# A planned order of work laid out anew: load times in the plan, the last step's product order, and the table of urgency shifts

## The chip, the cores and the metric

The kernel runs on one core of a Trainium2 chip. A core has five engines that work side by side, each through its own instructions in order: TensorE (matmuls into PSUM), VectorE and ScalarE (element by element), GpSimd (POOL in the profile), and SyncE (SP), whose queue here issues nearly all DMAs. The metric is the device time of one execution in microseconds; less is better. The program is one launch, and all loops are unrolled when it is built.

## The reference

Two blocks in a row, in float32. First a linear attention with decay (RWKV-6) for 4 batches, 8 heads, 768 steps, head width 48; then, over the heads laid side by side (384 wide), a layer norm and an MLP with a ReLU and a residual:

```
state = 0                                   # per batch and head, 48 x 48
for t in range(768):
    cur   = outer(u * k[t], v[t])
    y[t]  = r[t] @ (state + cur)
    state = w[t][:, None] * state + outer(k[t], v[t])
x   = y, heads side by side                 # (4, 768, 384)
xn  = (x - mean(x)) / sqrt(var(x) + 1e-6) * g_ln
out = x + max(xn @ w_ch1, 0) @ w_ch2        # w_ch1: 384 x 1536, w_ch2: 1536 x 384
```

## The kernel before

The work is cut into eight rounds, numbered 0 to 7: for each of the four batches two halves of 384 steps (RN). A round has three tiles of 128 steps (TT) and two units of four heads each (U). Round 0 is cut once more, into its first tile and the other two, so that work can start early.

A round's attention (`front`, line 1559 on) loads w, k, r and v, transposes w, k and r on TensorE (`turn`, tensors `w_ps`, `k_ps`, `r_ps`), and turns the recurrence into products inside chunks of 64 steps plus a state carried from chunk to chunk. Inside a chunk six levels (`quads`, `grow`, `keep`) alternate between many small matmuls that share the array (the "packed" groups, written to tensors called `a`) and VectorE, which multiplies k and r by decays (`tot`) and keeps the right squares under a mask. `states` computes the carried states, `outputs` the y, and `own` with `own_term` the term with u. In rounds 0 and 1 the loads put rows together in another way, so this last term goes through DRAM once (`own_by_tile`: `own_row` to `own_d` to `own`).

Then come the layer norm (`normalize`, `turn_x`) and the MLP (`first_product` for round 0, `mlp` for the others). The first product of a round has 12 parts f of 128 columns, the second adds 12 parts into three output tiles. To take fewer passes on TensorE than plain float32 does, operands are split into a high part, a low part and a difference: from round 1 on in the first product (`xhl`, `xd`, `wh`, `wl`, `d`), and in the last three rounds, 5 to 7, also in the second (`thirds`). There each f brings to each of the three output tiles i a product D of the differences (into one PSUM bank), and a product L and a product H (into another). For i = 0 and 1 the two banks are the two halves of one tile `a`; for i = 2 they are two tiles, `o_2D` and `o_2P`. Behind the last f VectorE adds D to x (`add`), then L + H to x (`rest`), and SP stores the tile (`store`).

What sets the order is the class `Plan` (line 67 on). The code above does not emit instructions; it calls `plan.add` with an engine, an assumed cost, the keys read and written, and an urgency `pri` (a smaller number goes first). The urgency of stage s in round n is 40n + s; MLP products lie 200 higher, so they fill in where the attention has nothing ready. `Plan.order` then plays through all operations: at each engine, among the operations that could start within WAIT of the earliest, it picks the one with the smallest urgency. The order in which it picks is the order of the program: each engine works through it, and waits where an input isn't there. So costs and urgencies in the plan have an effect on the chip through the order alone.

These parts matter here:

- `SHIFTS`: a table that adds a number to the urgency of all operations whose urgency has a given whole part. `MARGIN` is the delay assumed between an input and a packed group behind the first 60 us (FILLED); `PATIENCE` is how long GpSimd may be held for VectorE's shared port; `STAY` is a penalty on changing between packed and plain matmuls; `FETCH` the assumed time to fetch instructions; `WAIT` the window above, for each engine.
- `lat` is what the plan adds between an operation's end and the use of its result; for loads `size` is the time that the transfer takes up the DMA engines in the plan.
- `load` (line 494 on): rounds 0 and 1 (`ROWS`) take one DMA for each tensor and unit, later rounds three, one for each tile. The plan's cost for the three is 1.65, their latency 2.0. `load_v` (line 827 on) has the same latency.
- In `thirds` (line 1336 on), `go_d` issues the one matmul of D, `go` the two of L and H, `both` all three, in this order, as one planned operation of cost 0.525; its urgency is 200 + 40n + 2f + 3, which is 505 for the last f (11) of the last round.
- `idle` (line 1656 on) lets TensorE multiply zeros where the plan has a gap of more than 0.4 us in the first 90 us.

Of the kernel before, what the change touches and what calls it, by code (L numbers as in the profile page):

```python
# [35 lines left out]
class InOrder:  # L36


    waits, last = [], None
# [27 lines left out]
class Plan:  # L67
# [11 lines left out]

    HOP, MARGIN, FILLED, PATIENCE, STAY = 0.1, 0.196918, 60.0, 4.33011, 6.79752
    BEFORE, PIECE, FETCH, CROWD = 66, 256, 3.98109, 300
    WAITS = 1.006
    DRAIN = {True: 0.1, False: 0.12}
    WAIT = {"PE": 0.0354766, "ACT": 0.217982, "DVE": 0.140393, "POOL": 0.485775, "SP": 0.0207245}

    SHIFTS = {  # L90
        -537: -0.5, -535: -6.5, -520: -4, -457: -8, -337: 9.5, -296: 10.5, -295: 5.5, -200: -2,
        -38: -71, -34: 42.5, -31: -47, -30: -6.5, -29: 16, -25: -3, -18: -10.5, -14: -56, 0:
        -25, 6: -19.5, 8: -4, 9: -2.5, 10: -43, 11: 16, 12: -24, 14: 3, 16: 18, 17: 31, 26: -27,
        46: 6.5, 50: -49, 52: 46.5, 61: -28.5, 64: 5.5, 66: 11, 68: -8, 86: 5.5, 91: -28, 96:
        -20.5, 98: -50, 102: 40.5, 110: 4.5, 121: -4, 122: 14, 125: -0.5, 127: -9, 131: -17.5,
        136: -30, 140: 24.5, 165: -9, 166: -6, 168: -11.5, 172: -40, 174: -34.5, 178: -1.5, 180:
        -14.5, 182: 25.5, 202: 4.5, 203: 37, 204: -10, 210: -66.5, 212: -41, 260: -1.5, 261:
        -16.5, 280: 30, 283: -13, 284: -4.5, 310: 5, 319: -7.5, 320: 9, 402: 6, 407: -20.5, 409:
        -6, 411: -30, 418: -9.5, 425: 2.5, 440: -68, 442: 5, 443: 5.5, 444: -9.5, 450: -20.5,
        453: 38, 459: -24, 463: 40.5, 480: 3.5, 481: 3, 483: 9.5, 486: -3.5, 490: 3.5, 495: 15,  # L100
        496: 18, 497: 17.5, 499: 64.5, 501: 5,
    }

    def __init__(self, homes, dynamic):
# [37 lines left out]
    def order(self, busy, idle=None, until=0.0):  # L142
# [49 lines left out]
        def switching(t, op):  # L192
            drain = self.DRAIN[op.tiled] * (op.tiled != tiled)
            waits = fetches(t + drain, op)[0] > 2 * self.DRAIN[True]
            return self.STAY * (op.tiled != tiled) + self.CROWD * waits

        while todo:
            best = None
            for e, waiting in ready.items():
                at = [(t, op) for op in waiting if (t := start_of(op, e)) is not None]  # L200
                if not at:
                    continue
                first = min(t for t, _ in at)
                t, op = min(
                    ((t, op) for t, op in at if t <= first + self.WAIT[e]),
                    key=lambda x: (x[1].pri + (switching(*x) if e == "PE" else 0), x[1].i),
# [74 lines left out]
def kernel(  # L281
# [13 lines left out]
    PE, ACT, DVE, POOL, SP = (  # L295
        InOrder(tc, e) for e in (nc.tensor, nc.scalar, nc.vector, nc.gpsimd, nc.sync)
    )
# [8 lines left out]
    U = H // NH  # L306
# [11 lines left out]
    NR = B * NHALF  # L318
# [17 lines left out]
    plan = Plan(HOMES | {"a": 2, "b": 4}, ("a", "b"))  # L336
# [27 lines left out]
    ROWS, ROW = 2, TT * D  # L364
# [64 lines left out]
    def at(rnd, stage):  # L429
        return 40 * rnd + stage  # L430
# [13 lines left out]
    def urgent(part, stage):  # L444
        rnd, c0, nc = part
        return at(rnd - (nc == 1), stage)
# [47 lines left out]
    def load(nm, q):  # L494
        b, f, g = units[q]
        name = f"nat_{nm}{q}"

        def go():
            to = tile_("nat", name, None)
            if q // U < ROWS:  # L500
                SP.dma_start(
                    out=to[:, 0 : NH * ROW].rearrange("p (h x) -> p h x", h=NH),
                    in_=SRC[nm][b, ts(g, NH), ds(f * RN, RN)]
                    .rearrange("h (p c) d -> p h (c d)", p=P),
                )
                return
            for c in range(TT):
                SP.dma_start(
                    out=by_tile(to)[:, c, :, 0:D],
                    in_=SRC[nm][b, ts(g, NH), ds(f * RN + c * P, P)].rearrange("h p d -> p h d"),  # L510
                )

        cost_, size = (0.5, 1.05) if q // U < ROWS else (1.65, 1.6)
        plan.add(
            "SP", cost_, go, w=[name], new=[("nat", name)], pri=at(q // U, "wrk".index(nm)), lat=2.0,
            size=size,
        )

    def by_tile(t):
        return t.rearrange("p (c h d) -> p c h d", c=TT, h=NH)  # L520
# [306 lines left out]
    def load_v(q, part):  # L827
        _, c0, nc = part
        b, f, g = units[q]
        name, swapped = f"v{q}", f"vx{q}"  # L830

        def go():
            t = tile_("v", name, [P, NH, TT, D])
            for c in range(c0, c0 + nc):
                SP.dma_start(
                    out=t[:, :, c],
                    in_=v[b, ts(g, NH), ds(f * RN + c * P, P)].rearrange("h p d -> p h d"),
                )

        def swap():  # L840
            t, src = tile_("vx", swapped, [P, NP, TT, D]), tiles[name]
            cols = slice(c0 * D, (c0 + nc) * D)
            for i in range(2):
                SP.dma_start(
                    out=t[ds(C * (1 - i), C)].rearrange("p r c d -> p r (c d)")[..., cols],
                    in_=src[ds(C * i, C)]
                    .rearrange("p (r j) c d -> p r j (c d)", j=2)[:, :, 1, cols],
                )

        share = nc / TT  # L850
        plan.add(
            "SP", 0.1 + 1.6 * share, go, w=[(name, c0)], new=[] if c0 else [("v", name)],
            pri=urgent(part, 16), lat=2.0, size=1.6 * share,
        )
        plan.add(
            "SP", 1.3, swap, r=[(name, c0)], w=[(swapped, c0)], new=[] if c0 else [("vx", swapped)],
            pri=urgent(part, 17), lat=2.2, size=0.2 + 0.5 * share,
        )
# [477 lines left out]
    def thirds(rnd, f):  # L1336

        x_, h_, (g, c) = f"x{rnd}", f"h{rnd}_{f}", divmod(f, KC + 1)
        b, f0 = rounds[rnd]
        H_, L_, D_ = (f"h{n}{rnd}_{f}" for n in "HLD")  # L1340
        pri = at(rnd, FILL) + 2 * f + 3

        def out_tiles(i):
            if i < 2:
                t = tile_("a", f"o{rnd}_{i}", None)
                return t[:, 0, 0:RN], t[:, 1, 0:RN]
            return [tile_("b", f"o{rnd}_{i}{n}", [P, RN]) for n in "PD"]
# [21 lines left out]
        first, last = f == 0, f == FC - 1  # L1369
        whole = x_of(rnd)  # L1370
        for i in range(TT):
            o = f"o{rnd}_{i}"
            names = [o] if i < 2 else [o + "P", o + "D"]

            def go_d(i=i):
                PE.matmul(
                    out_tiles(i)[1], tiles[D_][:, ts(i, P)], tiles[f"w2d{f}"], start=first, stop=last
                )

            def go(i=i):  # L1380
                to = out_tiles(i)[0]
                PE.matmul(
                    to, tiles[L_][:, ts(i, P)], tiles[f"w2l{g}"][:, c], start=first, stop=False
                )
                PE.matmul(
                    to, tiles[H_][:, ts(i, P)], tiles[f"w2h{g}"][:, c], start=False, stop=last
                )

            def both(i=i):
                go_d(i)  # L1390
                go(i)

            def add(i=i):
                x = tiles[x_][:, i]
                DVE.tensor_tensor(
                    out=x, in0=out_tiles(i)[1].rearrange("p (h d) -> p h d", d=D), in1=x, op=ALU.add
                )

            def rest(i=i):
                x = tiles[x_][:, i]  # L1400
                DVE.scalar_tensor_tensor(
                    out=x, in0=out_tiles(i)[0].rearrange("p (h d) -> p h d", d=D),
                    scalar=1.0 + E12, in1=x, op0=ALU.mult, op1=ALU.add,
                )

            def store(i=i):
                SP.dma_start(
                    out=out[b, ds(f0 * RN + i * P, P), :].rearrange("t (h d) -> t h d", d=D),
                    in_=tiles[x_][:, i],
                )  # L1410

            keys = [o + n if i == 2 else (o, n) for n in "PD"]
            need = [H_, L_, D_, f"w2d{f}", (f"w2h{g}", c), (f"w2l{g}", c)]
            if first:
                need += x_of(NR - 1)
            plan.add(
                "PE", 0.525, both, count=6, r=need, w=keys,
                new=[("a" if i < 2 else "b", n) for n in names] if first else [],
                pri=pri, lat=0.17,
            )  # L1420
            if last:
                plan.add("DVE", 0.53, add, r=[keys[1]] + whole, w=[(x_, "sum", i)], pri=EVICT)
                plan.add("DVE", 0.53, rest, r=[keys[0], (x_, "sum", i)], w=[(x_, "out", i)], pri=EVICT)
                plan.add("SP", 0.36, store, r=[(x_, "out", i)], pri=EVICT, lat=2.0, size=0.65)
# [134 lines left out]
    def front(part):  # L1559
# [26 lines left out]
        if rnd:  # L1586
            for q in qs:
                load("r", q)
# [39 lines left out]
    def back(rnd):  # L1628
# [5 lines left out]
        w=["g"], pri=-10, lat=2.0, size=0.2,  # L1634
# [63 lines left out]
```

## Time and profile before

| | |
|---|---|
| median of 3 runs | 527.17 us (525.99 to 527.70) |
| profiled execution | 526.92 us |
| its span | 525.2 us |
| TensorE busy | 515.8 us (98%), 8996 matmuls in the records |
| VectorE busy | 403.6 us (77%) |
| ScalarE busy | 269.8 us (51%) |
| GpSimd busy | 72.2 us (14%) |
| DMA | 55.84 MB, mean 106 GB/s |
| granted TensorE clock | 1.00 |

The profile is of one execution. The span runs from the first to the last instruction; the time of the execution has some 1.7 us more around it. Names in its lines are the program's: `nat<-in_r_dram` is a load of r, `r_ps` the transposed r, `a<-r,k` packed squares, `idle<-nought` the multiplied zeros, `x<-a,x` an addition into the output. All instructions carry line 50, that of a helper that records them, so one goes by the names. "idle before <-releaser" is time in which the engine had nothing running, and what ended it. A matmul's end is modelled, and matmuls overlap: neighbours of 128 x 384 start about 0.175 us apart, though each is shown with 0.33 us and more.

### The profile page before, as it was taken

The page shows a single profiled execution, that of the slowest core. Times are in us where ns is not written, and L with a number is a line of the kernel's source. Part 1 is how long each engine was busy: PE and PEld are TensorE (multiplying, and loading weights), DVE is VectorE, ACT ScalarE, POOL GpSimd, SP SyncE. Part 2 cuts the span into 40 slices and gives each one's busy share as a digit, 9 for nine tenths or more (in the row PEclk, how much of TensorE's full clock was granted, in tenths as well). Part 3 has the DMA queues.
Part 4 walks back from the last instruction along what each step waited for, and adds up shares of the span by engine and source line. Part 5 has one row for each costly group of instructions (what it writes and reads, how often), then busy time and mean ns, then how long its engine had stood idle before and what let it go on. Part 6 is the DMA issues. An engine that isn't in the chain of part 4 may idle for free.

```text
span 525.2 us, 20616 instructions
## 1 busy us (share of the span) xinstructions
PE 515.8 (98%) x8996; PEld 434.5 (83%) x8996; DVE 403.6 (77%) x845; ACT 269.8 (51%) x602; POOL 72.2 (14%) x106
## 2 busy tenths in 40 slices
PE   9999999999999999999999999999999999999996
PEld 6788788677998668989777898669967999999996
DVE  5899988998899998999893886736664855855645
ACT  3788978973584244385451395246731524332221
POOL 7311311100420012223120010001500000000000
PEclk9999999999999999999999999999999999999999
DMA  9958595087545724655712311404101322322201
GB/s 215 273 158 205 119 232 163 18 208 209 143 83 102 187 50 93 145 121 102 174 39 67 78 38 25 133 22 120 47 16 61 107 61 65 101 60 85 83 0 46
DMA packets 122362, 55.84 MB, mean 106 GB/s; under 512 B 93984, under 2 KB 119200, under 8 KB 122272
## 3 DMA queue, kind: packets, MB, share of 16 engines
q1 hardware_dynamic: 119152, 53.54, 40.3%
q10 hardware_dynamic: 3120, 0.98, 1.0%
q8 instruction: 71, 1.16, 0.9%
q14 instruction: 19, 0.16, 0.1%
HBM read 45.05 MB, written 7.10 MB: 99 GB/s over the span
## 4 chain that ended last, share of the span: by engine, by line
PE 88%; DMA 4%; DVE 3%; POOL 2%; ACT 1%; issue 0%; SPq 0%; POOLq 0%; DVEq 0%
PE a L50 24%; PE o L50 23%; PE h_ps L50 21%; PE hd_ps L50 9%; PE o_2P L50 2%; PE w_ps L50 2%; PE r_ps L50 2%; DMA nat<-in_w_dram 2%; PE kn_ps L50 2%; PE k_ps L50 2%; PE xT_ps L50 1%; PE o_2D L50 1%; DVE x L50 1%; DMA own<-own_d 1%; DVE w L50 1%; POOL wide L50 1%
## 5 line engine op out<-in xcount | busy, mean ns | idle before, releaser
L50 PE MATMUL o<-ffn,h 128*128 128x384 f32 x360 | 124.4, 490 | 0.0
L50 PEld LDWEIGHTS o<-ffn,h 128*128 128x128 f32 x360 | 65.7, 190 | 37.5
L50 ACT COPY h<-hd_ps 128x384 f32<-128x384 f32 x84 | 40.3, 479 | 80.0 <-PE hd_ps L50 77.4
L50 DVE SCALAR_TENSOR_TENSOR h<-h_ps,h 128x384 f32<-128x384 f32 x84 | 46.5, 555 | 42.1 <-PE h_ps L50 38.1
L50 PEld LDWEIGHTS a<-r,k 48*60 48x60 f32 (+5 forms) x4608 | 63.3, 126 | 15.4 <-issue 7.4
L50 PE MATMUL a<-r,k 48*60 48x32 f32 (+5 forms) x4608 | 69.6, 212 | 0.9 <-issue 0.6
L50 PE MATMUL h_ps<-xhl,wl 128*128 128x384 f32 x252 | 61.1, 350 | 0.0
L50 PE MATMUL h_ps<-xhl,wh 128*128 128x384 f32 x252 | 57.6, 337 | 0.0
L50 PE MATMUL hd_ps<-xd,d 128*128 128x384 f32 x252 | 57.2, 348 | 0.0
L50 DVE TENSOR_TENSOR k<-k,tot 112x768 f32<-112x768 f32 (+1 forms) x50 | 41.7, 833 | 16.7 <-PE a L50 13.9
L50 PEld LDWEIGHTS hd_ps<-xd,d 128*128 128x128 f32 x252 | 44.2, 188 | 1.6 <-ACT w L50 0.2
L50 PEld LDWEIGHTS h_ps<-xhl,wl 128*128 128x128 f32 x252 | 43.8, 188 | 1.8 <-DVE h L50 0.2
L50 PEld LDWEIGHTS h_ps<-xhl,wh 128*128 128x128 f32 x252 | 45.2, 188 | 0.0
L50 ACT ACTIVATE h<-h 128x384 f32<-128x384 f32 x48 | 25.1, 525 | 33.3 <-DVE h L50 32.7
L50 DVE TENSOR_TENSOR r<-r,tot 112x768 f32<-112x768 f32 (+1 forms) x50 | 40.3, 807 | 0.0
L50 DVE COPY_PREDICATED A<-mask,a 128x768 f32<-128x768 int8 (+2 forms) x36 | 39.3, 1091 | 0.5 <-PE a L50 0.3
L50 ACT ACTIVATE hH<-h 128x384 fp32r<-128x384 f32 x36 | 18.4, 524 | 30.2 <-DVE h L50 25.8
L50 ACT COPY A<-a 32x384 f32<-32x384 f32 (+2 forms) x36 | 15.5, 432 | 26.9 <-PE a L50 25.7
L50 DVE SCALAR_TENSOR_TENSOR hL<-h,hH 128x384 fp32r<-128x384 f32 x36 | 19.9, 553 | 9.8 <-ACT hH L50 9.7
L50 PE MATMUL h_ps<-xf,w 128*128 128x128 f32 (+1 forms) x144 | 26.2, 331 | 0.0
L50 PE MATMUL a<-w2d,hD 128*128 128x384 f32 x72 | 24.6, 342 | 0.7 <-DVE hD L50 0.7
L50 PEld LDWEIGHTS a<-v,A 64*64 64x64 f32 x384 | 20.5, 133 | 5.4 <-issue 2.0
(121 smaller groups left out, 1000.8 us busy)
## 6 DMA issues: line engine op xcount, KB each, us to landing
d<-w1d SPq DMA_DIRECT2D x84, 192.0 KB, 2.9
raw<-in_moe_w_ch_dram SPq DMA_DIRECT2D x24, 384.0 KB, 4.7
v<-in_v_dram SPq DMA_DIRECT2D x48, 96.0 KB, 2.8
out_dram<-x SPq DMA_DIRECT2D x24, 192.0 KB, 1.9
nat<-in_w_dram SPq DMA_DIRECT2D x36, 96.0 KB, 3.5
nat<-in_k_dram SPq DMA_DIRECT2D x36, 96.0 KB, 3.6
nat<-in_r_dram SPq DMA_DIRECT2D x36, 96.0 KB, 3.1
w1d<-w1diff SPq DMA_DIRECT2D x12, 192.0 KB, 2.7
```

The costliest lines, as they stand in the source:

```text
L50: ins = self.tc.keep_in_program_order(f(*args, **kw))
```

## The change

Three things change, and with the third some constants of the planner. The plan's cost of a group of three loads goes from 1.65 to 1.95 and their latency from 2.0 to 2.5 (rounds 2 to 7); that of `load_v` from 2.0 to 2.5 in all rounds. In the last f of the last round, the three D products are planned as operations of their own, with an urgency lower by 100, and the L and H products as others. The table SHIFTS is replaced, 92 entries by 60, and MARGIN, PATIENCE, STAY, FETCH and WAIT have new values.

```diff
-    HOP, MARGIN, FILLED, PATIENCE, STAY = 0.1, 0.196918, 60.0, 4.33011, 6.79752
-    BEFORE, PIECE, FETCH, CROWD = 66, 256, 3.98109, 300
+    HOP, MARGIN, FILLED, PATIENCE, STAY = 0.1, 0.05, 60.0, 15.1983, 20.0356
+    BEFORE, PIECE, FETCH, CROWD = 66, 256, 3.72835, 300
...
-    WAIT = {"PE": 0.0354766, "ACT": 0.217982, "DVE": 0.140393, "POOL": 0.485775, "SP": 0.0207245}
+    WAIT = {"PE": 0.0403625, "ACT": 0.191784, "DVE": 0.109619, "POOL": 0.0526016, "SP": 0.0742572}
...
     SHIFTS = {
...
+        -280: 9, -217: 13, -40: 14, -19: 28, -6: 19.5, 0: 8, 1: -20.5, 5: -18, 6: -131.5, 11:
+        -21, 16: -8, 18: -18.5, 38: -9.5, 42: 5, 48: -51.5, 52: -22.5, 58: -28, 61: -5, 64: -42,
+        67: -35, 88: 4.5, 98: -23, 120: -1, 130: -51, 131: 13, 136: -3, 162: 3.5, 170: -9, 172:
...
+        423: 52, 441: 13, 448: 6, 451: 114.5, 452: -3.5, 453: 12, 455: 15, 465: -2.5, 480: -32,
+        489: 49, 493: 18.5, 499: 9, 502: 10.5,
     }
...
-        cost_, size = (0.5, 1.05) if q // U < ROWS else (1.65, 1.6)
-        plan.add(
-            "SP", cost_, go, w=[name], new=[("nat", name)], pri=at(q // U, "wrk".index(nm)), lat=2.0,
+        cost_, size = (0.5, 1.05) if q // U < ROWS else (1.95, 1.6)
+        plan.add(
+            "SP", cost_, go, w=[name], new=[("nat", name)], pri=at(q // U, "wrk".index(nm)), lat=2.0 if q // U < ROWS else 2.5,
             size=size,
...
-            pri=urgent(part, 16), lat=2.0, size=1.6 * share,
+            pri=urgent(part, 16), lat=2.5, size=1.6 * share,
...
-            plan.add(
-                "PE", 0.525, both, count=6, r=need, w=keys,
-                new=[("a" if i < 2 else "b", n) for n in names] if first else [],
-                pri=pri, lat=0.17,
-            )
+            if last and rnd == NR - 1:
+
+                plan.add("PE", 0.18, go_d, count=2, r=need, w=keys[1:], pri=pri - 100, lat=0.17)
+                plan.add("PE", 0.36, go, count=4, r=need, w=keys[:1], pri=pri, lat=0.17)
+            else:
+                plan.add(
+                    "PE", 0.525, both, count=6, r=need, w=keys,
+                    new=[("a" if i < 2 else "b", n) for n in names] if first else [],
+                    pri=pri, lat=0.17,
+                )
```

## The prediction

> **What bounds the kernel now.** I read the busy shares of the page first, then busy time by stretch, TensorE's waits, the chain that ended last, and the timeline at both ends.
>
> Busy time by stretch (columns: stretch, length, busy time and number of operations of each engine, granted clock, DMA share, GB/s):
>
> ```profile
> 0.00:75.00 75.00, 70.93 (x1469) 58.45 (x1471) 64.09 (x156) 56.02 (x132) 24.68 (x56) 1.00 0.80 197
> 75.00:275.00 200.00, 200.00 (x4704) 161.11 (x4705) 182.50 (x372) 116.12 (x261) 33.91 (x36) 1.00 0.54 126
> 275.00:375.00 100.00, 100.00 (x1887) 81.34 (x1886) 66.21 (x142) 49.19 (x110) 11.78 (x14) 1.00 0.24 64
> 375.00:525.20 150.20, 144.87 (x946) 133.63 (x945) 90.84 (x178) 48.47 (x102) 1.86 (x2) 1.00 0.21 64
> ```
>
> Between 75 and 375 us TensorE is never idle in the records; what another order can win lies at the two ends. Of the 5.33 us missing after 375, 0.7 is one wait and 4.7 is the tail (last matmul ends at 520.18 + 0.34 = 520.5, span 525.2). The front misses 4.07 us, and part of its 70.93 busy is filler: `idle` matmuls of zeros. TensorE's waits from 60 us on (waiter, releaser: us in total, times, longest):
>
> ```profile
> PE r_ps L50 <- DMA nat<-in_r_dram: 0.7, 1, 0.7
> PE a L50 <- DVE hD L50: 0.7, 1, 0.7
> PE xT_ps L50 <- DVE xn L50: 0.4, 1, 0.4
> ```
>
> The only load that TensorE waits for is one load of `r`, at 72 us. The filler behind the first 8 us, in the timeline of TensorE (start, length):
>
> ```profile
> 19.73 0.70 PE L50 MATMUL idle<-nought 128*128 128x256 f32 x2
> ...
> 20.86 1.14 PE L50 MATMUL idle<-nought 128*128 128x384 f32 x4
> ...
> 22.31 1.78 PE L50 MATMUL idle<-nought 128*128 128x384 f32 x6
> ...
> 29.92 1.35 PE L50 MATMUL idle<-nought 128*128 128x384 f32 x4
> ```
>
> With three shorter pieces (24.31: 0.82, 28.17: 0.49, 32.29: 1.25) this is 7.5 us of filler; with the 3.1 us that TensorE is idle between 8 and 75 (67.00 less 63.92), 10.6 us of the front are no work. But VectorE is busy 59.1 of those 67 us, and from 20 to 75 us 51.0 of 55: where its chain sets the pace, a new order can win some 4 us at the very most.
>
> **Loads planned longer.** From round 2 on, one `load` is three DMA issues. The code costs the group at 1.65 us of SP's queue and 2.0 us of latency, after the change at 1.95 and 2.5 (`load_v`: latency alone). No instruction is added; the planner only believes that the data come 0.8 us later and puts the transposes accordingly. In the trace such groups hold SP's queue for 1.47 to 3.34 us, and their DMAs land 3.1 (r) to 3.6 us (k) after issue, so the new figures are nearer to the trace. What they can win is what is lost to late loads: 0.7 us, at most 1.2 (the weight load's wait for the same r). I take -0.7. Where transposes are put 0.8 us later, first and second MLP products cover it (TensorE has no gap from 75 us on), so the cost is nothing; without that cover it is 0.8 us in each of six rounds, 4.8 us. At 75 to 275 us VectorE is 91% busy and has little to catch up with; I keep 0 to +0.8 of this for the range.
>
> **D products first.** In the last step (round 7, f = 11) the order per output tile was D, L, H; now the three D products get urgency 405 in place of 505, and L, H keep 505. The count of matmuls (nine) is the same, near 0.175 us each; no DMA moves. What can move is the row of six additions behind them:
>
> ```profile
> 518.26 0.33 PE L50 MATMUL a<-w2d,hD 128*128 128x384 f32 x1
> ...
> 518.60 0.34 PE L50 MATMUL a<-w2h,hH 128*128 128x384 f32 x1
> ...
> 518.98 0.56 DVE L50 TENSOR_TENSOR x<-a,x 128x384 f32<-128x384 f32 x1 [1.39 <-PE a L50]
> ...
> 519.57 0.56 DVE L50 SCALAR_TENSOR_TENSOR x<-a,x 128x384 f32<-128x384 f32 x1
> ...
> 521.75 0.56 DVE L50 SCALAR_TENSOR_TENSOR x<-o_2P,x 128x384 f32<-128x384 f32 x1
> ```
>
> The six run from 518.98 to 522.31 without a break over 0.1, so VectorE, not TensorE, sets the end: what counts is when the first starts. Its input is D alone, over at 518.26 + 0.33 = 518.59; it started at 518.98, 0.04 after H (518.94). In the program the wait is thus for the whole two-bank tile `a`, though D and L/H lie in different banks. The Trainium skill, "PSUM — Partial Sum Buffer", section "Summary: rules for kernel authors", asks only for a different bank, guarded by bank. By that rule nothing in the new order waits: hD of f = 11 is ready at 517.60, the two first D go at 517.73 and 517.90 (their f = 10 parts are done by then), the additions start 0.37 after the first, at 518.10, and end at 521.45: -0.86. By the row, the dependence is on the whole tile, and so probably also in reverse: L of tile 0 waits for the addition that reads D of tile 0, and that of tile 1 too. Then addition 0 takes 518.10 to 518.66, addition 1 518.7 to 519.25; TensorE meanwhile has tile 2 of f = 10 and its D (0.7 us), then L0 at 518.78, unhindered; L1 waits from 519.13 to 519.29; H1 is over at 519.80; the four remaining additions run 519.34 to 521.65: **-0.65**, which I take. The store behind the last addition (landing 1.9 us) moves with it. Bad end: if f = 10 is wholly done when D comes (first D at 518.79), L0 stands at TensorE's head until addition 0 is over, half a microsecond, addition 1 waits for H1, 1.85 us after D, and the last five additions end at 518.79 + 4.7 = 523.5: +1.2.
>
> **Shifts and planning constants.** 92 entries of SHIFTS are replaced by 60 others, and MARGIN, PATIENCE, STAY, FETCH and WAIT change. They add no instruction, but any operation and any DMA on every queue can change place, SP's and POOL's too; the trace of before cannot show the new order. Bounds: a gain up to the 4 us of VectorE's free time at the front plus 0.7 (the wait for hD); below nothing as much, since no reason excludes a worse front: -4.7 to +4. I take -0.9, a fifth of the gain, because the row nearest to it is SP's queue at the front, where one thing is visibly out of place:
>
> ```profile
> 43.81 1.90 SPq L50 DMA_DIRECT2D raw<-in_moe_w_ch_dram  x1
> 45.80 1.49 SPq L50 DMA_DIRECT2D nat<-in_k_dram  x3
> 47.33 0.51 SPq L50 DMA_DIRECT2D own<-own_d  x1
> ```
>
> `own` comes back from DRAM in 4.05 us on the chain that ended last, and three loads of k (1.49 us) stood in front of it; TensorE's idle time from 50 to 75 us is 1.7 us (0.50 and 1.24), so putting that right is worth between 0 and 1.5. The rest of SHIFTS I put at nothing on balance: entry 38 (-9.5) brings the conversion of the MLP weights forward, -6 (+19.5) holds VectorE's part of the first six back, 6 (-131.5) brings round 0's first products of w forward; all three work on the front's VectorE, against each other.
>
> MARGIN falls from 0.197 to 0.05: packed matmuls (quads, states, outputs) are planned 0.147 us closer to their inputs. There are 10 such groups in each of rounds 1 to 7: 70 x 0.147 = 10.3 us if each were hit in full. The chain shows a VectorE result (ending 29.28) used by TensorE at 29.33, a handoff of about 0.04, inside 0.05. With groups on TensorE of about 1 us, one in seven starts in the window and then half of it late: 70 x 0.147 x 0.07 = 0.7; I take +0.1 and keep 0 to 0.7. STAY from 6.8 to 20 can join packed groups: two joined output groups take 2.95 us against 2 x 1.55 apart, 0.15 each; ten joins would be -1.5, I take none. PATIENCE lets POOL wait longer for VectorE's port; POOL is busy 14% and its waiters have slack, except at the front.
>
> **Sum.** -0.7 - 0.65 - 0.9 + 0.1 = -2.15 us. The profiled execution took 526.92 (span 525.2 and 1.7 around it); its sum gives 524.8. It lies 0.25 under the median of the runs shown, 527.17; against the median the result is **525.0 us**.
>
> **Rivals.** (1) *Nothing that counts changes.* The middle is full either way, one load stall moves elsewhere, and the tail's gain is lost to L0's wait (+1.2 in place of -0.65): -0.7 + 1.2 - 0.9 + 0.1 = -0.3, so 526.9. For it: 300 us without a gap. Against it: hD is late in the trace, so D of tile 0 would come early. (2) *Slower: the front's chain breaks on SP's queue.* SP is one queue in order; each load group set in front of `own` or of a round's first `w` costs 1.5 to 2.7 us of issue, and in the front TensorE has no other work. Two groups (1.5 + 2.0) turn -2.15 into +1.35; from there it decides, and with four at 1.9 it is -2.15 + 7.6 = +5.4: 532.6. For it: the raw and k issues above already delay `own`; longer loads make the planner issue loads earlier. Against it: only round 1 and 2 loads stand there. The Trainium skill, "TensorE: Matmul & The Clock Gate", section "Why this matters for your kernels", adds that a TensorE gap over about 3 us halves its clock. Here the longest wait is 1.0 and the clock 1.00 throughout, so by the row a hole costs only itself; by the rule one over 3 us behind 90 us, where the planner no longer fills with `idle`, costs about 1.7 more (half of an estimated 3.4 us window from that page): 534. (3) *Much faster*: VectorE's 4 us at the front all gained: -0.7 - 0.65 - 4 - 0.7 = -6, 521.1. For it: 7.5 us of filler; against: VectorE at 93% from 20 us on.
>
> **How the numbers follow.** The runs shown spread by 1.7 us, about 0.3%, which is what a measurement can tell from no change (1.6 us). Forecast (faster by 0.3 to 0.9%) 0.40; rival 3 0.08; rival 1 0.14; rival 2, any size, 0.38, since an order that is new throughout has many ways to be worse and I can't see it. So faster 0.48, same 0.14, slower 0.38. The range leaves out the best third of rival 3 and the outer part of rival 2: 520.5 to 533.0; the forecast's own is 522.5 to 525.6.
>
> **What would show it.** Right: no wait of r_ps for its load; the first addition of the tail under 0.4 us behind the first D, last matmul to last addition under 1.5 us (now 1.8); less than 7.5 us of filler. Wrong: `a` waiting for `x` on TensorE at the end; filler after 33 us or a TensorE idle share in 0 to 75 above 4.1 us; SP issues of loads directly in front of `own`; any TensorE idle time between 75 and 375.

## The result, and the profile after

The changed kernel takes **524.07 us** (median of 6 runs, 523.47 to 525.00) against 526.96 (6 runs, 525.81 to 527.70): 2.9 us less by the medians. The ratio, estimated from the single runs, is 0.9933 (95% interval 0.9913 to 0.9954), which would be 3.5 us. The profiled execution took 523.47, its span 521.6; the span of before was 525.2.

Busy time by stretch of the changed kernel (columns as before: stretch, length, busy time and number of operations of TensorE, its weight loads, VectorE, ScalarE, GpSimd; clock, DMA share, GB/s):

```profile
0.00:75.00 75.00, 72.06 (x1519) 60.13 (x1520) 62.38 (x155) 57.67 (x136) 22.12 (x54) 1.00 0.83 202
75.00:275.00 200.00, 199.50 (x4897) 160.86 (x4891) 181.97 (x374) 112.84 (x253) 37.03 (x38) 1.00 0.54 124
275.00:375.00 100.00, 100.00 (x1492) 81.24 (x1485) 58.71 (x121) 47.33 (x104) 12.00 (x13) 1.00 0.23 62
375.00:521.60 146.60, 142.53 (x1124) 132.19 (x1122) 94.46 (x196) 53.01 (x111) 1.02 (x1) 1.00 0.21 66
```

TensorE is idle for 2.9 us of the front instead of 4.1, and for 4.1 behind 375 instead of 5.3. Its waits (waiter, releaser: us in total, times, longest):

```profile
PE a L50 <- issue: 1.3, 3, 0.5
PE idle L50 <- DVE eps L50: 1.0, 1, 1.0
PE k_ps L50 <- PE idle L50: 0.7, 1, 0.7
PE r_ps L50 <- ACT xf L50: 0.2, 1, 0.2
```

No transpose waits for a load any more, and no `a` for hD. But the four waits in its first and third line, 2.06 us in all, end with nothing that released them (`k_ps` at 53.86 follows its own filler by 0.72 us); before had 0.56 us of that kind. The last section comes back to them. One of them, 0.43 us at 232.6, lies where before had no gap.

The tail in the timeline (start, length):

```profile
513.37 0.56 DVE L50 SCALAR_TENSOR_TENSOR hD<-hH,hL 128x384 fp32r<-128x384 f32 x1
...
514.52 0.51 PE L50 MATMUL a<-w2d,hD 128*128 128x384 f32 x2
...
514.89 1.02 DVE L50 TENSOR_TENSOR x<-a,x 128x384 f32<-128x384 f32 x2 [0.96 <-PE a L50]
...
515.50 0.19 PEld L50 LDWEIGHTS a<-w2l,hL 128*128 128x128 f32 x1 [0.27 <-DVE x L50]
...
516.16 0.56 DVE L50 SCALAR_TENSOR_TENSOR x<-a,x 128x384 f32<-128x384 f32 x1 [0.25 <-PE a L50]
...
517.04 0.56 DVE L50 SCALAR_TENSOR_TENSOR x<-a,x 128x384 f32<-128x384 f32 x1 [0.32 <-PE a L50]
...
517.19 0.34 PE L50 MATMUL o_2P<-w2h,hH 128*128 128x384 f32 x1
...
518.17 0.56 DVE L50 SCALAR_TENSOR_TENSOR x<-o_2P,x 128x384 f32<-128x384 f32 x1
```

Two additions follow the first two D at once. In return L of tile 0 waits 0.27 us for an addition that reads the other half of its tile, and VectorE twice waits for an H.

And SP's queue where the prediction looked for the front's gain:

```profile
44.16 1.52 SPq L50 DMA_DIRECT2D nat<-in_w_dram  x3
45.78 0.87 SPq L50 DMA_DIRECT2D own_d<-own_row  x1
48.10 1.47 SPq L50 DMA_DIRECT2D nat<-in_k_dram  x3
50.04 0.37 SPq L50 DMA_DIRECT2D own<-own_d  x1
```

`own` is issued at 50.04 instead of 47.33. The three loads of k still stand in front of it, but they no longer hold it: `own_d`, which it reads, lands only 4.2 us after its issue, at 49.98. In before it had landed at 45.56, and `own` went 1.77 us later. So the order did put right what the prediction had found; `own_row` is ready later instead, and the front won nothing here.

**Where the time went.** Since the order is new throughout, stretches of the two profiles don't hold the same work. So I worked out, for each profile, how far TensorE is *behind*: the time since the start, less the work begun by then, each matmul counted at its usual distance to the next of its kind in the trace of before (323 ns for a record of the plain second product, 176 for the split products, 109 and 96 for transposes, 112 and 216 for round 0's first product; packed matmuls by the group: a group of 96 squares 0.95 to 1.50 us by level, one of 48 states 0.69, one of 94 outputs 1.52; filler nothing). In every kernel this work adds up to 484.6 us. Behind, in us, at six times:

| | 60 | 75 | 275 | 375 | 420 | 500 |
|---|---|---|---|---|---|---|
| before | 21.1 | 23.9 | 31.1 | 34.3 | 35.7 | 35.7 |
| same order but for the last step (`d_alone_2`) | 20.0 | 22.7 | 30.1 | 33.4 | 34.6 | 34.6 |
| changed | 21.6 | 22.0 | 29.6 | 31.6 | 32.7 | 32.5 |
| changed but for the last step (`new_without_d`) | 21.2 | 21.5 | 29.1 | 31.3 | 32.4 | 32.3 |
| changed but for the last stretch (`new_no499`) | 21.6 | 22.6 | 30.7 | 32.9 | 34.1 | 33.9 |

Rows of the same order differ by 0.9 to 1.7 us from 75 us on, so a single pair of profiles doesn't do, and a gain of 1 us between two means is not far above that scatter. The means of the two old-order rows and the three new-order rows (33.85 and 31.9 at 375, and so on) give: 1.25 us won in the first 75 us, 0.4 lost again up to 275, 1.1 won from 275 to 375, 0.3 from there to 500. From the last matmul's end to the span's end it is 4.7 us in before, 4.1 changed. Together 2.2 + 0.6 = 2.8, close to the 2.9 of the medians.

Two of these stages can be read further. At 60 us the new order is not ahead but 0.9 behind; the front is won between 60 and 75 us (before, then changed):

```profile
60.00:75.00 15.00, 13.76 (x218) 11.21 (x212) 13.41 (x28) 12.21 (x30) 0.84 (x3) 1.00 0.93 223
60.00:75.00 15.00, 15.00 (x229) 13.32 (x228) 14.20 (x25) 12.70 (x33) 1.42 (x1) 1.00 0.86 218
```

There the old order waits for a load, 0.73 us for r in before, 1.32 for k in `d_alone_2`, and the new one doesn't. And from 275 to 375 TensorE waits for nothing in any of the 13 profiles that are read here, yet the new order loses 1.1 us less. What differs is how often it changes between packed and plain matmuls: 34 times in both old-order profiles (3.1 and 3.2 us lost), 23 or 24 times in the three new ones (2.0 to 2.2), 36 times in `new_fetch` (3.5). Over all 13 that is some 0.09 us a change, an estimate from a line through these points; no run changed their number alone.

### The profile page after: what moved, and what is told of

Read it like the earlier page. It is cut to its first block, busy times and chain, and to the rows that moved or that the text cites. A ratio compares the mean times of both kernels' runs of the same rounds, so it can differ in the third digit from the quotient of the medians.

```text
span 521.6 us, 20645 instructions
## 1 busy us (share of the span) xinstructions
PE 514.1 (99%) x8998; PEld 434.4 (83%) x8998; DVE 397.5 (76%) x844; ACT 270.8 (52%) x603; POOL 72.2 (14%) x106
## 4 chain that ended last, share of the span: by engine, by line
PE 97%; DVE 1%; ACT 1%; issue 1%; DVEq 0%
PE a L50 26%; PE o L50 22%; PE h_ps L50 22%; PE hd_ps L50 9%; PE w_ps L50 3%; PE k_ps L50 3%; PE r_ps L50 3%; PE idle L50 3%; PE o_2P L50 2%; PE kn_ps L50 2%; PE xT_ps L50 1%; PE o_2D L50 1%; DVE xhl L50 0%; DVE x L50 0%; DVE xd L50 0%
## 5 line engine op out<-in xcount | busy, mean ns | idle before, releaser
L50 PEld LDWEIGHTS a<-r,k 48*63 48x63 f32 (+5 forms) x4608 | 63.4, 126 | 15.9 <-issue 6.6
L50 PE MATMUL a<-r,k 48*63 48x32 f32 (+5 forms) x4608 | 69.6, 212 | 1.0 <-issue 0.9
L50 PE MATMUL h_ps<-xhl,wl 128*128 128x384 f32 x252 | 59.8, 345 | 0.0
L50 PE MATMUL hd_ps<-xd,d 128*128 128x384 f32 x252 | 55.5, 346 | 0.1
L50 DVE TENSOR_TENSOR k<-k,tot 112x768 f32<-112x768 f32 (+1 forms) x50 | 40.2, 805 | 18.8 <-PE a L50 18.5
L50 POOL TENSOR_TENSOR rk<-nat,nat 128x576 f32<-128x576 f32 (+1 forms) x13 | 17.8, 1368 | 74.9 <-PE a L50 19.7
L50 ACT COPY r<-r_ps 112x384 f32<-112x384 f32 (+1 forms) x31 | 14.2, 493 | 23.2 <-PE r_ps L50 23.1
```

Of the source, the lines that this page charges most:

```text
L50: ins = self.tc.keep_in_program_order(f(*args, **kw))
```

## The experiments

**The D products, in both directions.** Before with that part alone (`d_alone`, and the same edit once more as `d_alone_2`, whose profile is read here), and the changed kernel without it:

```diff
@@ before, to d_alone and d_alone_2
-            plan.add("PE", 0.525, both, count=6, ...)
+            if last and rnd == NR - 1:
+                plan.add("PE", 0.18, go_d, count=2, r=need, w=keys[1:], pri=pri - 100, lat=0.17)
+                plan.add("PE", 0.36, go, count=4, r=need, w=keys[:1], pri=pri, lat=0.17)
+            else:
+                plan.add("PE", 0.525, both, count=6, ...)
@@ changed, to new_without_d: the same lines the other way round
```

> The kernel before with one part of the change: the D products of the last step planned first. TensorE's order differs from that of before in its last stretch alone. Theory (the tail's sum of the prediction, with a wait on the whole two-bank tile): -0.65 us, the first addition starts within 0.4 us of the first D, and the L product of tile 0 or 1 shows a wait for an addition x of 0.1 to 0.3 us. Rival (a wait by bank only, as the rule has it): -0.86 us and no such wait. Rival (D first does nothing, since the additions wait for H anyway): 0.

> The kernel before with the D products of the last step first, once more for an undisturbed profile. In the changed kernel the same edit moved the stretch from the last hD to the last addition by +0.15 us only (4.80 with, 4.65 without), since L of tile 0 waits for an addition. Theory now: TensorE ends 0.1 to 0.3 us later than in before, counted from the last hD, the additions end 0.2 us earlier to 0.3 later; time within 0.3 us of before. Rival (the prediction's sum): -0.65 us from the last hD to the last addition (4.71 in before, so 4.06).

> The changed kernel with the last step's products in the old order (D, L, H in one piece); all else as changed. Theory: +0.5 to +0.65 us against the changed kernel, all behind the last step's first D, so still about -2.3 us against before. Rival (the tail is most of the gain): back to within 1 us of before.

Measured: `d_alone` 526.46 us (12 runs; ratio 0.9980, 0.9961 to 0.9998), `d_alone_2` 526.89 (ratio 0.9968, 0.9917 to 1.0019), `new_without_d` 523.41 (ratio 0.9937, 0.9913 to 0.9960, the changed kernel's own being 0.9933). The times leave between nothing and some 2 us for the edit in the old order and can't see it in the new one, where +0.5 us had been expected without it; so the tail is read in the profiles. The last hD in before, then the tail of `d_alone_2`:

```profile
517.04 0.56 DVE L50 SCALAR_TENSOR_TENSOR hD<-hH,hL 128x384 fp32r<-128x384 f32 x1
```

```profile
516.00 0.56 DVE L50 SCALAR_TENSOR_TENSOR hD<-hH,hL 128x384 fp32r<-128x384 f32 x1
...
516.70 0.33 PE L50 MATMUL o_2D<-w2d,hD 128*128 128x384 f32 x1
...
517.22 0.51 PE L50 MATMUL a<-w2d,hD 128*128 128x384 f32 x2
...
517.59 1.02 DVE L50 TENSOR_TENSOR x<-a,x 128x384 f32<-128x384 f32 x2 [1.03 <-PE a L50]
...
518.20 0.19 PEld L50 LDWEIGHTS a<-w2l,hL 128*128 128x128 f32 x1 [0.27 <-DVE x L50]
...
518.87 1.09 DVE L50 SCALAR_TENSOR_TENSOR x<-a,x 128x384 f32<-128x384 f32 x2 [0.25 <-PE a L50]
...
520.52 0.56 DVE L50 SCALAR_TENSOR_TENSOR x<-o_2P,x 128x384 f32<-128x384 f32 x1
```

hD is ready at 516.56, but the first D comes at 517.22, because the plan had put one more part of tile 2 (516.70) ahead of it; in before the distance was the same 0.66. From the last hD's end to the last addition's it is 4.71 in before and 4.52 here: **-0.19**. In the new order it is 4.65 without the part and 4.80 with it: **+0.15**, TensorE ending 0.22 later (3.61 for 3.39 behind hD) and the additions 0.07 sooner behind it. The lines of the new order without the part:

```profile
513.05 0.56 DVE L50 SCALAR_TENSOR_TENSOR hD<-hH,hL 128x384 fp32r<-128x384 f32 x1
...
516.65 0.34 PE L50 MATMUL o_2P<-w2h,hH 128*128 128x384 f32 x1
...
517.70 0.56 DVE L50 SCALAR_TENSOR_TENSOR x<-o_2P,x 128x384 f32<-128x384 f32 x1
```

So D first, by itself, is worth nothing that counts in these profiles, one of each kernel. The prediction's -0.65 is out, and so is its rival by banks, -0.86 with no wait of L: the 0.27 is there. The third rival had the amount, 0, but not the reason: the first addition does not wait for H, it starts 0.37 behind the first D (517.59 and 517.22). Most of the shorter tail is there without it: from the last matmul's end to the last addition's end 1.79 in before, 1.27 in `new_without_d`, 1.20 changed.

**The end of the table.** One entry of the last round taken out:

```diff
-        489: 49, 493: 18.5, 499: 9, 502: 10.5,
+        489: 49, 493: 18.5, 502: 10.5,
```

> The changed kernel without one entry of the table of shifts, 499: 9, which held back f = 8 of the last round; only the last stretch is ordered otherwise, so that the third tile's parts no longer come last and less stands between the L and H of tiles 0 and 1. Theory: additions wait less for H, the last addition ends 0.0 to 0.3 us earlier relative to the last matmul; time 0 to -0.3 us against the changed kernel. Rival (what is gained there is lost to L's wait for an addition): +0.1 to +0.5 us.

523.56 us, ratio 0.9940 (0.9914 to 0.9966), no change in time. The theory, up to 0.3 us less, missed: in its profile hD to last addition takes 4.97 (4.80 changed), last matmul to last addition 1.37 (1.20): tile 2 now keeps up, and less of it is left to put between the products of tiles 0 and 1. That is the rival's +0.1 to +0.5, though in one profile.

**The load times alone, and the rest without them.**

```diff
@@ before, to loads_alone; changed, to new_old_loads: the other way round
-        cost_, size = (0.5, 1.05) if q // U < ROWS else (1.65, 1.6)
+        cost_, size = (0.5, 1.05) if q // U < ROWS else (1.95, 1.6)
...
-            pri=at(q // U, "wrk".index(nm)), lat=2.0,
+            pri=at(q // U, "wrk".index(nm)), lat=2.0 if q // U < ROWS else 2.5,
...
-            pri=urgent(part, 16), lat=2.0, size=1.6 * share,
+            pri=urgent(part, 16), lat=2.5, size=1.6 * share,
```

> The kernel before with the longer load times in the plan alone; table, constants and last step as before. The order differs from about round 1 on. Theory of the prediction: the 0.7 us wait of r_ps for its load at 72 us is gone, no other load wait comes in its place; -0.7 us at that place, and elsewhere the table fits the plan less well, 0 to +3 us. Rival (the load figures do nothing for the chip): the wait of r_ps or of another transpose for a load is still there, 0.5 us or more.

> The changed kernel with the old, shorter load times in the plan. Theory (a load that is planned too early is waited for): a wait of TensorE for a load or for the transposes' copies of 0.5 us or more comes back between 60 and 275 us, +0.7 to +1.2 us there, and up to +3 more from an order that the table wasn't made for. Rival (the table alone made the gain): no such wait, within 0.7 us of the changed kernel.

`loads_alone`: 529.83 us, ratio 1.0022 (0.9964 to 1.0080). `new_old_loads`: 534.73, ratio 1.0113 (1.0052 to 1.0175). TensorE's waits for loads in the first and in the second:

```profile
PE r_ps L50 <- DMA nat<-in_r_dram: 0.7, 1, 0.7
...
PE k_ps L50 <- DMA nat<-in_k_dram: 0.2, 1, 0.2
```

```profile
PE r_ps L50 <- DMA nat<-in_r_dram: 0.8, 2, 0.5
...
PE k_ps L50 <- DMA nat<-in_k_dram: 0.2, 1, 0.2
```

With the longer times alone r is waited for as before, at 77.5 us: the rival's case. With the old times under the new table waits for r return, 0.8 us at 167 us, as expected; but `new_old_loads` falls some 11 us back against the changed kernel by 275 us, far more than the 1 to 4 us expected. Loads are the smaller part of it. The waits that nothing released are 6.4 us, against 2.1 in the changed kernel:

```profile
PE a L50 <- issue: 3.7, 6, 1.1
PE o L50 <- issue: 1.6, 1, 1.6
PE k_ps L50 <- issue: 1.1, 1, 1.1
```

Two stretches at half clock cost up to 3.4 us more (see the last section). The old order is itself not steady here: `d_alone_2`, the same until the last step, waits 1.3 us for a load of k at 69 us and none for r. None of the profiles with the new early order (changed, `new_without_d`, `new_no499`, `new_fetch`) shows a transpose waiting for a load. But `new_patience` and `new_no_early`, further down, do, by 1.9 and 1.5 us, and they too plan with the longer times. The wait belongs to the order, then, and the load figures do not remove it by themselves.

**What any other order costs.** One constant moved by 0.6%, and each half of the table left out:

```diff
@@ changed, to new_fetch
-    BEFORE, PIECE, FETCH, CROWD = 66, 256, 3.72835, 300
+    BEFORE, PIECE, FETCH, CROWD = 66, 256, 3.75, 300
@@ changed, to new_no_early: SHIFTS keeps its 28 entries from 200 on
@@ changed, to new_no_late: SHIFTS keeps its 32 entries below 200
```

> The changed kernel with a planning constant moved by a hair (FETCH 3.72835 to 3.75), which means nothing for the chip but makes the plan choose otherwise from early in round 0 on: a measure of what an arbitrary other order costs. Theory that the changed kernel's gain is mostly a well-found order: slower than the changed kernel by 1 to 5 us. Rival (the gain comes from the load figures and the last step, not from this order): within 0.7 us of the changed kernel.

> The changed kernel with the entries of the table below 200 left out, that is without shifts for the attention of rounds 0 to 4 and for the conversion of weights; the entries from 200 on stay. Theory (the table's gain in the first 75 us is the largest single part, 1.9 of 3.6 us): that lead is gone, TensorE's work at 75 us is behind that of the changed kernel by 2 to 6 us. Rival (the front is bound by VectorE whatever the order): within 1 us at 75 us, and what is lost is lost later.

> The changed kernel without the entries of the table from 200 on, that is without shifts for the attention of rounds 5 to 7 and for all MLP products; the early entries stay. Theory (from 275 us on the late entries win 1.2 us by fewer changes between packed and plain matmuls, and 0.9 by having hD ready when the second product of round 5 starts): work done at 75 us as in the changed kernel within 0.7 us, then more changes (over 30 between 275 and 400) or a wait for hD of 0.5 us or more, +1 to +3 us in all. Rival (late entries are without effect): within 0.7 us of the changed kernel.

`new_fetch`: 525.48 us, ratio 0.9979 (0.9961 to 0.9997), 1.4 above the changed kernel by the medians, 2.4 by the two ratios: the theory's 1 to 5. Its front is the changed kernel's (21.6 behind at 75), its loss of some 2 us comes from 275 to 420, with 36 changes between packed and plain groups before 375 and a 1.1 us wait for hD. `new_no_early`: 538.07, ratio 1.0177 (1.0112 to 1.0241); 26.4 behind at 75, that is 4.4 more than changed, inside the theory's 2 to 6, and another 11 by 275. `new_no_late`: 531.16, ratio 1.0075 (1.0041 to 1.0108); 22.1 behind at 75, level with changed (within 0.4) until 250, 4.2 behind it at 500. By the medians it is 7 us slower, where +1 to +3 was expected. The line of its waits that bears on it:

```profile
PE a L50 <- DVE hD L50: 2.0, 2, 1.1
```

Changes between packed and plain groups, which the theory also named, were not it: 30 from 275 to 400, against 31 in the changed kernel and 36 in before. So without the early entries most is lost, without the late ones hD comes too late, and an order that nobody looked for is worse by 1.4 us in the mildest case. Such losses, 14 and 7 us, are far above the 2.9 us that the whole change wins: they say what an unfitted order costs, not what each half of the table contributes.

**PATIENCE and MARGIN.** In before some VectorE operations took twice their time. In the timeline of before, not shown ahead:

```profile
22.45 0.42 DVE L50 TENSOR_TENSOR k<-k,tot 112x256 f32<-112x256 f32 x1
22.52 1.22 POOL L50 TENSOR_TENSOR rk<-nat,nat 128x384 f32<-128x384 f32 x1 [0.30 <-DVE tot L50]
22.80 1.23 DVE L50 TENSOR_TENSOR r<-r,tot 112x256 f32<-112x256 f32 x1
```

`r` takes as long as `k`, 0.42, except here, where it lasts until GpSimd's product is over: +0.81. The same happens at 14.7 (+0.65), 43.9 (+0.76) and 51.9 (+0.65): 2.9 us of VectorE's time in the front. In the changed kernel the groups of the first 75 us read (line, engine, operation, count, busy and mean ns):

```profile
L50 DVE TENSOR_TENSOR k<-k,tot 112x256 f32<-112x256 f32 x15 | 6.3, 421 | 1.5 <-PE a L50 1.5
L50 DVE TENSOR_TENSOR r<-r,tot 112x256 f32<-112x256 f32 x15 | 6.3, 420 | 0.0
```

None is slow (486 and 471 ns on average in before). PATIENCE is the constant by which the plan holds GpSimd back for VectorE, so it was put back, and set alone; MARGIN likewise put back:

```diff
@@ changed, to new_patience
-    HOP, MARGIN, FILLED, PATIENCE, STAY = 0.1, 0.05, 60.0, 15.1983, 20.0356
+    HOP, MARGIN, FILLED, PATIENCE, STAY = 0.1, 0.05, 60.0, 4.33011, 20.0356
@@ before, to old_patience: PATIENCE 4.33011 becomes 15.1983
@@ changed, to new_margin
-    HOP, MARGIN, FILLED, PATIENCE, STAY = 0.1, 0.05, 60.0, 15.1983, 20.0356
+    HOP, MARGIN, FILLED, PATIENCE, STAY = 0.1, 0.196918, 60.0, 15.1983, 20.0356
```

> The changed kernel with the old PATIENCE (4.33 in place of 15.2), so that GpSimd may again take the port that it shares with VectorE after a shorter wait. Theory (new): part of the front's gain comes from VectorE's two-input operations no longer running beside GpSimd's; in before four of them between 14 and 54 us took 0.65 to 0.81 us more than alone, 2.9 in all, in the changed kernel none. So here one to four such slow operations come back in the first 75 us, TensorE's work at 75 us is 0.5 to 3 us behind the changed kernel; the time is 1 to 6 us above it, the table not being made for it. Rival (PATIENCE plays no part, as the prediction had it): no slow operation in the first 75 us, and the same work done at 75 us within 0.5 us.

> The kernel before with the new PATIENCE alone (15.2 in place of 4.33). Theory: VectorE's slow operations, 12 of them with 7.5 us over their time alone in before, become half or fewer from the point on where the order differs; the time itself may go either way by 3 us, since the table isn't made for it. Rival: as many slow operations as before.

> The changed kernel with the old MARGIN (0.197 in place of 0.05). Theory of the prediction (the smaller margin costs TensorE some 0.1 us in short waits of packed groups): TensorE's waits of packed groups between 75 and 400 us are no fewer than 0.1 us apart in the sum from the changed kernel's, and the time is 0 to 4 us above it through the other order alone. Rival (the smaller margin costs much, up to 10 us, and is paid for elsewhere): waits of packed groups fall by 1 us or more.

`new_patience`: 537.91 us, ratio 1.0186 (1.0132 to 1.0241). One slow operation of that size comes back in the front (54.1 us, +0.65) and two of +0.3, and TensorE is 23.6 behind at 75, 1.6 more than changed: the numbers that the theory expected. That the one makes the other is not shown, since TensorE is level with the changed kernel at 60 us (21.6 both). Most of its loss (14 us) lies from 75 to 275. `old_patience`: 539.69, ratio 1.0224 (1.0169 to 1.0279); it has 11 operations more than 0.15 us over their usual time, 5.6 us in all, against 12 and 7.5 in before. Half or fewer was expected: missed. So PATIENCE alone does not clear the collisions; that none is left in the front is seen only with the whole new set of table and constants. How much of the front's 1.25 us is due to that stays open; all four lie ahead of 60 us, where the new order has no lead yet. `new_margin`: 529.01, ratio 1.0044 (1.0014 to 1.0074). TensorE's waits at packed groups sum to 1.2 us, to 1.3 in the changed kernel, and to 0.1 and 0.4 in the stretch from 75 to 400 that the expectation named: the smaller margin costs nothing that can be seen, and the large cost of the rival is out. Most of the 5 us is lost between 125 and 275, to another order.

## Why the prediction was right

Forecast 525.0 us and -2.15 against the median shown; measured 524.07 and -2.9. Direction, range and likeliest case (522.5 to 525.6) held. That the sum came out near is luck in good part: of its three gains one is right in amount and not in cause, one is not there, and the third is larger than forecast and lies elsewhere. All the signs that the prediction named against itself can be found in the profile: `a` waits for `x` (0.27), filler comes after 33 us, loads of k are issued directly in front of `own`, and TensorE is idle between 75 and 375 (0.43). Of the signs for it, the one on filler failed. Of its terms:

- **Loads, -0.7.** The wait of r_ps is gone, so the amount stands; the reason does not. The longer times alone left it in place (`loads_alone`), and it is the whole new order that avoids it. It is part of the front's 1.25, which arises where the old order waits for it.
- **D first, -0.65.** Failed. The step that failed is "the two first D go at 517.73 and 517.90", 0.13 behind hD. The plan puts one more part ahead of them: they start 0.66 behind hD in the old order, 0.60 in changed, 1.12 in `new_no499`. By the planner's own rule a lower urgency counts only among operations that could start by then, so the plan must have believed hD later than the parts that it put first; the plan's own times stand in no profile. The reverse wait was foreseen and is there: 0.27 at L of tile 0, where by the rule on banks alone there would be none. Measured -0.19 in the old order, +0.15 in the new.
- **Shifts, -0.9.** Too small and laid in the wrong place. The front won 1.25 including the load, not through `own` on SP's queue. The step behind it, "what another order can win lies at the two ends", because TensorE has no gap from 75 to 375, did not hold: 1.1 us were won from 275 to 375, where neither order has a gap, along with 11 fewer changes between packed and plain matmuls. Not foreseen either were 0.3 us behind 375, where the wait for hD (0.7 in before) is gone, and the shorter tail through the order of the tiles, 0.5 us. That VectorE at 93% leaves the front little was right in kind: the front gained far less than 4.
- **Filler.** "Less than 7.5 us" was wrong: it is 8.5 us by TensorE's busy time, with new pieces at 45.3, 48.9, 52.0 and 59.4 us. From each filler matmul's start to the next start, without the wait at 53.86, it is 7.6 us, to 6.9 in before. Filler says how the plan fills its gaps, not how long they are.
- **MARGIN, +0.1.** Nothing was seen. STAY's joins, put at none, are a term left out that may have counted: 83 changes became 76 between 75 and 275, without a gain there, but 34 became 23 between 275 and 375, with 1.1 us. How many of these are due to STAY and how many to SHIFTS is not shown.

Of the rivals, SP's queue did not break. Rival 2's thought that a new order has many ways to be worse has some footing now: of the eight other orders tried on either base that differ well before the last stretch, six came out slower than before with the whole interval above 1, one is open (`loads_alone`), and only the one moved by a hair stayed faster. They were made by breaking a fitted order, though, so they give no chance for a change that was meant to help.

## What to carry to other kernels

A planner's cost, its constants and its table of shifts make one order, and are worth something together only: to test one of them, compare stages of the profiles, since the time of the whole mostly tells what an unfitted order costs. Where an engine is full, look for the gain at both ends, but also at how often it changes between kinds of work, since a trace without a gap can still lose time there; and take several profiles of one order before believing 1 us of it. An operation moved ahead in priority starts sooner only if what it needs is believed ready, and if its tile isn't shared with what comes next.

## What the runs showed that was not expected

**Waits that nothing released end behind a transfer of code.** In the 13 profiles that are read here (all but that of `d_alone`) TensorE waits 53 times (0.15 us or more, 32 us in all) where no semaphore explains it, like the `issue` and `k_ps` lines of the changed kernel. The page lists a DMA queue that carries instructions (queue, kind: transfers, MB, share):

```profile
q8 instruction: 71, 1.16, 0.9%
```

In the DMA records of the trace these are 71 transfers of 16 KB, one for about every 254 of TensorE's records. All 53 waits end 2.2 to 2.8 us after such a transfer starts; if they had nothing to do with each other, about one in eight would. The three in the dense work around 18, 53 and 58 us recur in most profiles of the new order. So these are very probably waits for instructions, which is what the plan's FETCH (3.7 to 4.0 us) stands for; no run moved a transfer alone, so it is not shown by experiment. They are 0.6 us in before, 2.1 in the changed kernel and 6.4 in `new_old_loads`, a cost of an order that the prediction had no term for.

**TensorE's clock fell at small holes.** The prediction quoted a limit of about 3 us of idleness. In `new_old_loads` (stretch, length, busy of each engine, clock, DMA), and the wait inside it:

```profile
93.00:96.80 3.80, 2.79 (x194) 2.55 (x193) 3.27 (x6) 3.77 (x9) 0.00 (x0) 1.00 0.02 4
96.80:100.20 3.40, 2.79 (x5) 1.58 (x5) 3.40 (x7) 1.47 (x4) 0.00 (x0) 0.50 0.00 0
100.20:104.00 3.80, 3.80 (x22) 2.63 (x22) 1.72 (x4) 2.36 (x6) 0.00 (x0) 0.99 0.19 56
```

```profile
97.41 3.49 PE L50 MATMUL o<-ffn,h 128*128 128x384 f32 x6 [1.61 <-issue]
```

Behind one hole of 1.61 us (95.79 to 97.41), and 1.0 of it ahead of the change, the clock stands at one half for 3.41 us. It did so at 59.3 us in the same profile (1.13 us idle in the 3.4 us ahead), in `new_no_early` (1.21) and in `new_patience` (1.8); each such time costs up to 1.7 us, half of its 3.41. It did not in `loads_alone` and `d_alone_2` (1.33) nor in `old_patience` (1.43), so no single figure for the limit follows; behind the first 9 us no 3.4 us hold more than 0.87 in before and 0.72 in changed. Holes far below 3 us can thus cost double.

**A late load shows up as a slow VectorE operation.** In `new_no499` the work is that of the changed kernel until the last stretch, yet `k<-k,tot` took 2.20 us at 223.8 (0.95 alone), and a packed group then waited 1.14 us. GpSimd's product of r and k ran beside it, from 223.79 on, because the last load of r landed at 223.54; in the changed kernel it landed at 220.37, and the product (from 220.95 on) was over before `k<-k,tot` began at 223.08. What GpSimd overlaps depends on when things land, so the plan's avoidance of collisions holds only as far as its times do.
